# Chunk 0 of a recurrence with five idle products a pair instead of eight, and six weight tiles loaded in halves

## The chip, the core and the metric

The kernel runs on one NeuronCore of a Trainium2 chip. The metric is the time of one execution on the device in microseconds; before the change its median over three runs is 486.32 us. The engines are TensorE (PE, with its weight loads shown as PEld), VectorE (DVE), ScalarE (ACT), GpSimd (POOL) and SyncE (SP), which issues nearly all DMAs.

## What is computed

A linear recurrence over 768 tokens with a state of 48 x 48 for each of 4 x 8 heads, and behind it a two-layer network on its outputs:

```
for t in range(S):                              # S = 768
    cur = einsum('bhd,bhe->bhde', u * k[t], v[t])
    y[t] = einsum('bhd,bhde->bhe', r[t], state + cur)
    state = w * state + einsum('bhd,bhe->bhde', k[t], v[t])
x = y as (3072 tokens, 384)
h = x @ w_in                                    # 384 x 2048
g = maximum(h, 0) + alpha * minimum(h, 0)
out = g @ w_out                                 # 2048 x 384
```

All in float32. The kernel multiplies each float32 matrix as a sum of a high and a low half, three products for one (wh with xh, wl with xh, wh with xl).

## The kernel before

The tokens are cut into six chunks of 128 for each of the four batches (512 columns), the eight heads into four pairs. For each chunk, the recurrence of each pair is done with products inside the chunk and through a state carried from chunk to chunk; its output goes, split into xh and xl, into the tiles that the network reads. The network runs in steps: one step is one block of 128 of the 2048 hidden features for one chunk. A step issues nine products of the first matrix (`m_in`, L678), the leaky function on ScalarE and VectorE (L686 to L691), and nine products of the second matrix (`m_out`, L712) into three accumulators. Steps 0 to 8 are chunk 0 with weights 0 to 8, steps 9 to 17 chunk 1 with the same weights, steps 18 to 24 chunk 0 with weights 9 to 15, then the rest.

Weights arrive as 64-bit floats, 768 KB a block (`raw_weights`, L323, two buffers), and are turned into a high and a low float32 half by ScalarE and VectorE (`weights`, L343 to L354): L353 writes the high half, L354 the low one.

Chunk 0 (`first_chunk`, one call for each pair) runs before step 0: sums for the diagonal (L507, copied by L511), scores (L442), ScalarE's copies of a scaled identity (L449, eight a pair), VectorE's merging of the scores (L453), the outputs (L463) and, in `state`, transposes (L295, copied by L299) and state products (L489). The outputs of a pair are split by L389, L390 and L392, those of the last pair by L378 and L379. The first pair has its outputs in a tile of its own, from which `lower` (L367) moves twelve strips of 16 rows to where the products of step 0 read them: k = 0, 1, 2, high and low, two each, on SP's queue.

An idle product multiplies the identity by itself into the accumulator acc2, which nobody reads (`warm`, L233). `with_warm(n, ...)` issues n of them ahead of a group of real products, and a piece of 23 stands at the program's start.

The order of the instructions on each engine is not written by hand. Every piece of work is added with an engine, a cost in microseconds, its reads and writes and a rank, and the planner (`in_order`) places them one after the other by these costs, which include 0.16 for an idle product; where a hole of more than 0.25 us is left on TensorE ahead of the network, it fills it with idle products. So a change of an early cost can move work on all engines. Each of the engines then executes its queue in order.

DMAs take eight completion semaphores in turn (DMAHW0 to DMAHW7); a DMA waits for the one eight places before it. At the end, in the branch that is taken when the check of the inputs passed (the line number is that of the `If`, L840), SP waits for each of the eight, from DMAHW0 to DMAHW7, one instruction each, and then goes to the closing barrier. The check itself is a product (L775) and a few VectorE operations, up to L781.

## Time and profile before

| | us |
|---|---|
| median of three runs (lowest, highest) | 486.32 (486.30, 486.80) |
| the profiled execution, on the device | 486.93 |
| its span, from the first to the last instruction | 485.2 |
| TensorE busy | 476.6 (98%) |
| VectorE busy | 310.8 (64%) |
| ScalarE busy | 247.2 (51%) |
| GpSimd busy | 43.5 (9%) |

An engine's busy time counts its instructions from start to end. TensorE's are pipelined, so a row's duration there holds some overlap with the next; the distance from one row's start to the next row's start is what it takes in the queue. In a timeline the text in brackets is the idle time of the engine before the row and what ended it.

### The profile page before, as it was taken

The numbers are of one execution on the slowest core, as the hardware profiler recorded it, in microseconds if no ns is written. First come the engines' busy times: TensorE is split into PE (matmuls) and PEld (weight loads), VectorE is DVE, ScalarE is ACT, GpSimd is POOL, SyncE is SP. The second block draws the span as 40 slices with busy tenths as digits, with TensorE's granted clock in tenths as the row PEclk, the third lists the DMA queues.
The fourth block names the chain that finished last, engine by engine and source line by source line (L and its number), as shares of the span: only waits on it lengthen the run. The fifth ranks groups of instructions, "written<-read, shape, count | busy, mean of one in ns | idle before, by whom it ended". The sixth has DMA issues, their size and how long they took to land.

```text
span 485.2 us, 11237 instructions
## 1 busy us (share of the span) xinstructions
PE 476.6 (98%) x4644; PEld 387.5 (80%) x4644; DVE 310.8 (64%) x518; ACT 247.2 (51%) x578; POOL 43.5 (9%) x49
## 2 busy tenths in 40 slices
PE   8999999999999999999999999999999999999994
PEld 5778878888888888888888888888888878888883
DVE  7789999999786785855755655745644534333331
ACT  5889866776555552553553643444642333433222
POOL 2000010012211011101202202202000000000000
PEclk9999999999999999999999999999999999999998
DMA  8675776642243641431121341121210000100002
GB/s 238 193 209 187 225 242 190 228 157 66 72 131 106 187 136 57 136 103 36 58 83 37 118 119 37 54 75 33 95 26 1 1 1 0 67 0 0 1 1 70
DMA packets 23752, 45.82 MB, mean 94 GB/s; under 512 B 3856, under 2 KB 11408, under 8 KB 23696
## 3 DMA queue, kind: packets, MB, share of 16 engines
q1 hardware_dynamic: 23552, 44.92, 29.6%
q8 instruction: 38, 0.62, 0.6%
q14 instruction: 18, 0.15, 0.1%
q10 hardware_dynamic: 144, 0.13, 0.1%
HBM read 36.38 MB, written 6.29 MB: 88 GB/s over the span
## 4 chain that ended last, share of the span: by engine, by line
PE 88%; DVE 7%; ACT 2%; DMA 1%; issue 1%; POOL 0%; ACTq 0%; DVEq 0%; POOLq 0%
PE acc L712 40%; PE bank L678 38%; PE bank L612 2%; PE acc L233 2%; PE bank L622 2%; PE bank L591 2%; PE bank L584 1%; DVE wl L354 1%; DMA wraw<-wall 1%; DVE wx L350 1%; DVE wx L347 1%; DVE g L687 1%; DVE wx L345 1%; DVE gl L691 1%; ACT wx L343 1%
## 5 line engine op out<-in xcount | busy, mean ns | idle before, releaser
L687 DVE SCALAR_TENSOR_TENSOR g<-bank,alph,g 128x512 f32<-128x512 f32 x96 | 71.9, 748 | 107.0 <-ACT g L686 106.3
L686 ACT ACTIVATE g<-bank 128x512 f32<-128x512 f32 x96 | 57.3, 597 | 137.0 <-PE bank L678 136.5
L678 PE MATMUL bank<-xh,wh 128*128 128x512 f32 x288 | 113.0, 392 | 0.0
L678 PE MATMUL bank<-xh,wl 128*128 128x512 f32 x288 | 112.2, 390 | 0.1
L678 PE MATMUL bank<-xl,wh 128*128 128x512 f32 x288 | 112.1, 389 | 0.0
L691 DVE TENSOR_TENSOR gl<-g,gh 128x512 fp32r<-128x512 f32 x96 | 69.5, 724 | 41.6 <-ACT gh L690 41.4
L690 ACT ACTIVATE gh<-g 128x512 fp32r<-128x512 f32 x96 | 60.5, 630 | 66.1 <-DVE g L687 65.9
L712 PE MATMUL acc<-gh,wh 128*128 128x512 f32 x288 | 83.6, 396 | 0.0
L712 PE MATMUL acc<-gh,wl 128*128 128x512 f32 x288 | 82.0, 391 | 0.0
L712 PE MATMUL acc<-gl,wh 128*128 128x512 f32 x288 | 81.7, 390 | 0.0
L678 PEld LDWEIGHTS bank<-xh,wh 128*128 128x128 f32 x288 | 54.0, 188 | 11.6 <-ACT kk L299 0.3
L678 PEld LDWEIGHTS bank<-xh,wl 128*128 128x128 f32 x288 | 54.1, 188 | 11.5 <-DVE wl L354 0.5
L678 PEld LDWEIGHTS bank<-xl,wh 128*128 128x128 f32 x288 | 54.1, 188 | 11.3
L712 PEld LDWEIGHTS acc<-gl,wh 128*128 128x128 f32 x288 | 54.0, 188 | 11.3
L712 PEld LDWEIGHTS acc<-gh,wl 128*128 128x128 f32 x288 | 53.8, 188 | 11.4
L712 PEld LDWEIGHTS acc<-gh,wh 128*128 128x128 f32 x288 | 52.7, 188 | 11.2
L547 POOL TENSOR_TENSOR rr<-rr,kk 128x384 f32<-128x384 f32 x16 | 22.5, 1405 | 286.2 <-DMA kk<-vkr 227.1
L558 ACT ACTIVATE base<-ident,cu 128x64 f32<-128x64 f32 x160 | 41.5, 337 | 1.0 <-DVE cu L553 0.9
L379 DVE TENSOR_TENSOR xl<-bank,xh 48x256 fp32r<-48x256 f32 (+1 forms) x66 | 28.4, 430 | 1.5
L533 DVE TENSOR_TENSOR raw<-raw,W 112x512 f32<-112x512 f32 x40 | 26.7, 682 | 0.8 <-DMA raw<-rk 0.8
L378 ACT ACTIVATE xh<-bank 48x256 fp32r<-48x256 f32 (+1 forms) x66 | 25.5, 386 | 2.5 <-PE bank L622 1.0
L643 DVE COPY_PREDICATED base<-strict,bank 128x256 f32<-128x256 uint8 x40 | 17.3, 442 | 4.4 <-PE bank L591 4.4
(102 smaller groups left out, 388.2 us busy)
## 6 DMA issues: line engine op xcount, KB each, us to landing
wraw<-wall SPq DMA_DIRECT2D x16, 768.0 KB, 4.7
raw<-rk SPq DMA_DIRECT2D x46, 224.0 KB, 3.9
v<-vkr SPq DMA_DIRECT2D x24, 192.0 KB, 3.6
rr<-vkr SPq DMA_DIRECT2D x16, 192.0 KB, 2.5
kk<-vkr SPq DMA_DIRECT2D x16, 192.0 KB, 3.4
oT<-o SPq DMA_DIRECT2D x12, 256.0 KB, 2.2
oT<-g SPq DMA_DIRECT2D x5, 256.0 KB, 2.8
xh<-xh SPq DMA_DIRECT2D x36, 32.0 KB, 2.0
```

Of the source, the lines that this page charges most:

```text
L378: add("ACT", us, lambda: nc.scalar.activation(to(h), view(), AF.Copy), r=[src], w=refs(h), rank=rank)
L379: add("DVE", us + 0.1, lambda: nc.vector.tensor_tensor(out=to(l), in0=view(), in1=to(h), op=ALU.subtract), r=[src] + refs(h), w=refs(l), r ...
L533: add("DVE", 0.72, lambda t=t, tab=tab: nc.vector.tensor_tensor(out=t().rearrange("p b (j t) -> p (b j) t", t=span), in0=t().rearrange("p ...
L547: add("POOL", 1.2, lambda: nc.gpsimd.tensor_tensor(out=rt(), in0=rt(), in1=k(), op=ALU.mult), r=[k] + ([wh[12]] if c == 2 else []), w=[rt] ...
L558: add("ACT", 0.32, lambda g=g, b=b: nc.scalar.activation(base()[:, g, b], ident2(), AF.Copy, scale=cu()[:, g, b:b + 1]), r=[cu, ident2], w ...
L643: add("DVE", 0.42, lambda g=g: nc.vector.copy_predicated(base()[:, g], strict2()[:, None, :].broadcast_to([128, B, HI]), A[g]()[:, 0:256]. ...
L678: nc.tensor.matmul(hp()[:, :], a[i]()[:, k], x[c]()[:, k], start=(k == 0 and j == 0), stop=(k == NK - 1 and j == 2))
L686: add("ACT", 0.6, lambda: nc.scalar.activation(g(), hp()[:, :], AF.Copy), r=[hp], w=[g], rank=n - 100)
L687: add("DVE", 0.75, lambda: nc.vector.scalar_tensor_tensor(out=g(), in0=hp()[:, :], scalar=alph()[:, i:i + 1], in1=g(), op0=ALU.mult, op1=A ...
L690: add("ACT", 0.64, lambda: nc.scalar.activation(gh(), g(), AF.Copy), r=[g], w=[gh], rank=n - 100)
L691: add("DVE", 0.73, lambda: nc.vector.tensor_tensor(out=gl(), in0=g(), in1=gh(), op=ALU.subtract), r=[g, gh], w=[gl], rank=n - 99)
L712: nc.tensor.matmul(banks[k](), a[i]()[:, NK + k], x(), start=(begin and j == 0), stop=(end and j == 2))
```

## The change

Three things are changed. In `first_chunk`, `with_warm` gets 1 instead of 2 for the scores and for the outputs, and 0 instead of 1 for the state products; the sums for the diagonal keep 2, the transposes 1. The opening piece issues five idle products of 512 columns, one into each of the five rotating banks, and then 16 of 384 into acc2, instead of 23 of 384; the helper is split into `idle` and `warm` for that. And weights 10 to 15 are loaded by two DMAs of 384 KB each instead of one of 768 KB.

In the changed program 43 idle products are issued instead of 55: 41 by these parameters, and two that the planner puts ahead of the first transposes of chunk 1 (L295), of which two groups now stand ahead of step 0 instead of one. Ahead of every step's first product TensorE's queue otherwise holds the same products as before from step 3 on, apart from a few that change places with a neighbour, and apart from the check's product, which now stands far behind them. Lines of the changed file are higher by 3 to 10.

```diff
--- before.py
+++ after.py
@@ -229,9 +229,12 @@
 
 
     def warm(into):
-        x = ident().bitcast(mybir.dt.bfloat16)
-        nc.tensor.matmul(into()[:, 128:512].rearrange("p (a f) -> p a f", a=2), x[:, 0:128],
-                         x[:, None, 0:192].broadcast_to([128, 2, 192]), start=True, stop=True, skip_group_check=True)
+        idle(into()[:, 128:512])
+
+    def idle(into):
+        x, n = ident().bitcast(mybir.dt.bfloat16), into.shape[1] // 2
+        nc.tensor.matmul(into.rearrange("p (a f) -> p a f", a=2), x[:, 0:128],
+                         x[:, None, 0:n].broadcast_to([128, 2, n]), start=True, stop=True, skip_group_check=True)
 
     def with_warm(n, us, fn, r, w, rank):
 
@@ -320,8 +323,14 @@
 
     def raw_weights(i, rank, behind=()):
         t = raws[i] = sb([128, 2 * DM, 2], "wraw", 2, U32)
-        p = load(t, lambda: nc.sync.dma_start(t().rearrange("p f a -> p (f a)"), wall[i].bitcast(U32)), 768, rank, behind)
-        return p
+        if i < NF - 6:
+            return load(t, lambda: nc.sync.dma_start(t().rearrange("p f a -> p (f a)"), wall[i].bitcast(U32)), 768, rank,
+                        behind)
+
+        for j in range(2):
+            load((t, j), lambda j=j: nc.sync.dma_start(
+                t()[:, DM * j:DM * (j + 1)].rearrange("p f a -> p (f a)"),
+                wall[i].bitcast(U32)[:, 2 * DM * j:2 * DM * (j + 1)]), 384, rank)
 
     def weights(i, need):
 
@@ -442,7 +451,7 @@
                     nc.tensor.matmul(A[g]()[:, b * L:(b + 1) * L], k0()[half(g), b], r()[half(g), b], start=(b == 0),
                                      stop=(b == B - 1), skip_group_check=True)
 
-        with_warm(2, 1.05, scores, r=[r, k0], w=A, rank=q - 90).after.add(first)
+        with_warm(1, 1.05, scores, r=[r, k0], w=A, rank=q - 90).after.add(first)
         base = [sb([128, B, L], "gl", 3, F32, mv) if q % 2 else sb([128, B, L], "base", 3) for _ in range(2)]
         for g in range(2):
             for b in range(B):
@@ -464,7 +473,7 @@
                         :, x * D:x * D + rows.stop - rows.start], base[g]()[:, b], start=b == 0,
                         stop=b == B - 1, skip_group_check=True)
 
-        last_out[:] = [with_warm(2, 0.95, out, r=[v] + base, w=[y], rank=q - 85)]
+        last_out[:] = [with_warm(1, 0.95, out, r=[v] + base, w=[y], rank=q - 85)]
         h, l, kx = x_tiles(0, q)
         if q < P - 1:
             splits_by_pe(kx, h, l, y, 0.6, q - 51.2)
@@ -489,7 +498,7 @@
                         nc.tensor.matmul(u_rows(U, 0)[rows, b], kt[:, x * D:x * D + rows.stop - rows.start], v()[:, x],
                                          start=(b == 0), stop=(b == B - 1), skip_group_check=True)
 
-            with_warm(1, 0.75, product, r=[k, v], w=[U], rank=-45 + q)
+            with_warm(0, 0.75, product, r=[k, v], w=[U], rank=-45 + q)
             T[q] = sb([112, B, D], "T", 9)
             add("ACT", 0.4, lambda t=T[q]: nc.scalar.activation(t(), u_rows(U, 0), AF.Copy, scale=w128()[:, q:q + 1]),
                 r=[U, w128], w=[T[q]], rank=0.5 * q + 0.2)
@@ -781,7 +790,8 @@
         add("DVE", 0.1, lambda: nc.vector.tensor_copy(flag(), total()), r=[total], w=[flag], rank=at)
 
 
-    add("PE", 6.7, lambda: [warm(bank) for _ in range(23)], r=[ident], w=[(bank, "warm")], rank=-1000)
+
+    add("PE", 6.7, lambda: [idle(t) for t in plan.banks] + [warm(bank) for _ in range(16)], r=[ident], w=[(bank, "warm")], rank=-1000)
 
     begins = {}
     for n, (c, i) in enumerate(STEPS):
```

The first place is ScalarE's queue in chunk 0, from the copies for the third and fourth pair on: L449 (L458 after) is the scaled identity, L389 (L398) the first split of an output, L299 (L302) the copy of transposes, L343 (L352) and L353 (L362) belong to weights 0. Before:

```order
L449 ACTIVATE base<-ident,cu 128x128
L449 ACTIVATE gl<-ident,cu 128x128 x4
L389 ACTIVATE xh_394<-bank_116 112x512
L343 ACTIVATE wx<-wraw 128x768
L449 ACTIVATE gl<-ident,cu 128x128 x2
L299 ACTIVATE kk<-bank_118 128x192 x2
L449 ACTIVATE gl<-ident,cu 128x128 x2
L389 ACTIVATE xh<-bank_117 112x512
L389 ACTIVATE xh<-bank_119 112x512
L299 ACTIVATE kk<-bank_120 128x192 x2
L353 ACTIVATE wh_81<-wx 128x768
L299 ACTIVATE kk<-bank_118 128x192 x2
```

After:

```order
L458 ACTIVATE gl<-ident,cu 128x128 x4
L352 ACTIVATE wx<-wraw 128x768
L458 ACTIVATE base<-ident,cu 128x128 x4
L458 ACTIVATE gl<-ident,cu 128x128 x3
L302 ACTIVATE kk<-bank_119 128x192 x2
L302 ACTIVATE kk<-bank_120 128x192 x2
L458 ACTIVATE gl<-ident,cu 128x128
L398 ACTIVATE xh_441<-bank_117 112x512
L398 ACTIVATE xh<-bank_118 112x512
L398 ACTIVATE xh<-bank_116 112x512
L401 ACTIVATE xl_468<-bank_117 112x512
L401 ACTIVATE xl<-bank_118 112x512
```

Ahead of the first split, L389 or L398, stand 28 copies of the scaled identity before and all 32 after, and the six copies of transposes of the first three pairs and weights 0's first copy have moved ahead of it too.

The second place is SP's queue from the first strip of chunk 0 on: L367 (L376) moves a strip, xh high and xl low; wraw is a load of weights, raw, v and rr are inputs of chunk 1 and 2. Before:

```order
L367 DMA xh<-xh_394 16x512 x4
L323 DMA wraw<-wall 128x1536
L367 DMA xh<-xh_394 16x512
L404 DMA raw<-rk 112x512
L367 DMA xh<-xh_394 16x512
L367 DMA xl<-xl_469 16x512 x6
L406 DMA v<-vkr 128x384 x2
L404 DMA raw<-rk 112x512 x2
L406 DMA v<-vkr 128x384 x2
L323 DMA wraw<-wall 128x1536
```

After:

```order
L413 DMA raw<-rk 112x512 x3
L327 DMA wraw<-wall 128x1536
L376 DMA xh<-xh_441 16x512 x4
L376 DMA xl<-xl_468 16x512 x2
L376 DMA xh<-xh_441 16x512
L376 DMA xl<-xl_468 16x512 x2
L376 DMA xh<-xh_441 16x512
L376 DMA xl<-xl_468 16x512 x2
L415 DMA v<-vkr 128x384 x4
L554 DMA rr<-vkr 128x384
L327 DMA wraw<-wall 128x1536 x3
```

The loads of chunk 1's inputs and of weights 2 have left the places between the strips; the twelve strips follow each other.

The third place is SP's last stores, with the semaphores that each waits for (the DMA semaphore named is also the one that the store then takes; the store of the other half of the last tile is on ScalarE's queue and takes the semaphore between, DMAHW0 before and DMAHW6 after). Before:

```order
L755 DMA oT<-o 128x512 [waits DMAHW3_49,Activation_49]
L755 DMA oT<-o 128x512 [waits DMAHW4_49,Activation_49]
L755 DMA oT<-g 128x512 [waits DMAHW5_49,Activation_49]
L755 DMA oT<-o 128x512 [waits DMAHW6_49,Activation_49]
L755 DMA oT<-o 128x512 [waits DMAHW7_49,Activation_49]
L748 DMA oT<-g 128x256 [waits DMAHW1_49,DVE_49]
```

After:

```order
L764 DMA oT<-o 128x512 [waits DMAHW1_49,Activation_49]
L764 DMA oT<-o 128x512 [waits DMAHW2_49,Activation_49]
L764 DMA oT<-g 128x512 [waits DMAHW3_49,Activation_49]
L764 DMA oT<-o 128x512 [waits DMAHW4_49,Activation_49]
L764 DMA oT<-o 128x512 [waits DMAHW5_49,Activation_49]
L757 DMA oT<-g 128x256 [waits DMAHW7_49,DVE_49]
```

The last two stores take DMAHW0 and DMAHW1 before, DMAHW6 and DMAHW7 after.

## Rows read from the trace of the kernel before

**Rows 1.** Busy time by stage: stretch, its us, engines busy (instructions), clock, DMA share, GB/s.

```profile
8.00:30.90 22.90, 22.90 (x316) 16.54 (x315) 18.81 (x33) 19.88 (x60) 0.00 (x0) 1.00 0.73 218
30.90:70.00 39.10, 38.43 (x626) 30.74 (x625) 38.66 (x62) 31.86 (x82) 2.23 (x2) 1.00 0.72 232
70.00:478.00 408.00, 408.00 (x3680) 336.80 (x3679) 247.84 (x411) 191.18 (x426) 38.54 (x30) 1.00 0.23 72
```

**Rows 2.** Timeline of the opening: start us, us, engine, line, operation, count, [idle before].

```profile
1.48 6.58 PE L233 MATMUL acc<-ident 128*128 128x384 bf16 x25 [1.48 <-POOL ident L257]
...
5.94 0.15 PEld L233 LDWEIGHTS <-ident 128*128 128x128 bf16 x1 [0.17 <-issue]
...
6.26 1.42 PEld L233 LDWEIGHTS <-ident 128*128 128x128 bf16 x9 [0.17 <-issue]
```

**Rows 3.** Timeline of TensorE (PE) in chunk 0 and step 0.

```profile
10.51 0.50 PE L233 MATMUL acc<-ident 128*128 128x384 bf16 x2
10.94 0.63 PE L507 MATMUL acc<-uw,g 112*64 112x2 f32 x16
...
21.13 0.55 PE L295 MATMUL bank<-ident,raw 112*128 112x112 f32 x4
...
28.52 0.34 PE L233 MATMUL acc<-ident 128*128 128x384 bf16 x1
28.78 0.67 PE L489 MATMUL bank<-v,kk 128*64 128x48 f32 x16
...
32.88 0.39 PE L678 MATMUL bank<-xl,wh 128*128 128x512 f32 x1
```

**Rows 4.** Timeline of ScalarE (ACT) in chunk 0.

```profile
12.25 2.15 ACT L449 ACTIVATE gl<-ident,cu 128x128 f32<-128x128 f32 x7
...
17.10 0.99 ACT L449 ACTIVATE base<-ident,cu 128x128 f32<-128x128 f32 x3 [0.91 <-PE bank L463]
18.58 0.18 ACT L511 ACTIVATE cu<-acc 128x8 f32<-128x8 f32 x1 [0.50 <-PE acc L233]
...
20.12 0.58 ACT L389 ACTIVATE xh<-bank 112x512 fp32r<-112x512 f32 x1
20.59 0.91 ACT L343 ACTIVATE wx<-wraw 128x768 f32<-128x768 f32 x1
...
21.99 0.52 ACT L299 ACTIVATE kk<-bank 128x192 f32<-128x192 f32 x2
```

**Rows 5.** Timeline of VectorE (DVE) and TensorE where weights 1 are first used.

```profile
32.13 0.69 DVE L533 TENSOR_TENSOR raw<-raw,W 112x512 f32<-112x512 f32 x1
...
33.60 0.95 DVE L354 TENSOR_TENSOR wl<-wx,wh 128x768 fp32r<-128x768 f32 x1
...
34.67 0.50 PE L678 MATMUL bank<-xh,wh 128*128 128x512 f32 x1
```

**Rows 6.** SP's issues (timeline); part 6 of the page: KB each, us to landing.

```profile
20.72 3.01 SPq L367 DMA_DIRECT2D xh<-xh  x4
...
26.56 3.78 SPq L367 DMA_DIRECT2D xl<-xl  x6
...
226.93 4.93 SPq L404 DMA_DIRECT2D raw<-rk  x2
...
xh<-xh SPq DMA_DIRECT2D x36, 32.0 KB, 2.0
```

**Rows 7.** Windows of L678 alone; one line's view of L354 (min/median/max ns, starts).

```profile
0.00:121.60 121.60, 41.21 (x162) 29.98 (x163) 1.00 0.62 194
121.60:150.50 28.90, 13.21 (x54) 10.14 (x55) 1.00 0.36 115
...
L354 DVE TENSOR_TENSOR wl<-wx,wh x16: 942/950/1759, 25.3 to 123.3; 128x768 fp32r<-128x768 f32 x16
```

**Rows 8.** The tail: SP's waits (us in total, times, longest); its instructions of line 840.

```profile
SPq L840 <- SPq L840: 3.3, 2, 3.0
...
L840 SPq EVENT_SEMAPHORE  x8: 17/17/17, 483.1 to 483.9; - x8
```

## The prediction

> **What bounds the kernel now.** I read the windows first, because a share of 98% for TensorE says nothing about which stage could be shortened. From 8.0 to 30.9 us, the stage in which chunk 0 goes through the recurrence, TensorE is busy in all of its 22.90 us; from 30.9 to 70 it is busy for 38.43 of 39.10; from 70 to 478 for 408.00 of 408.00 [rows 1]. So the end of the program is the sum of what TensorE issues, plus a stall of well under a microsecond, plus the tail behind the last product. Whatever leaves TensorE's queue and is not replaced by a wait shortens the run, wherever it stands.
>
> The second thing to see in the windows is who would be late next. VectorE is busy for 18.81 of 22.90 us in chunk 0 (4.1 us idle) and for 38.66 of 39.10 between 30.9 and 70: after chunk 0 it is full, and it is the engine that makes the weights' low halves. One pair of rows shows how close it runs: the low half of weights 1 is written from 33.60 for 0.95 us, to 34.55, and the step that multiplies by it starts at 34.67 [rows 5]. So TensorE is full, but with VectorE right behind it, and ScalarE in chunk 0 (19.88 of 22.90) not far off.
>
> Third, the timeline of TensorE in chunk 0: between nearly all groups of real products stand idle products into acc2, one or two. Fourth, the tail: SP's own waits behind the last store.
>
> **The change, part by part.**
>
> *Idle products.* The parameters give 2+2+2+1+1 = 8 a pair before and 2+1+1+1+0 = 5 after, so 12 fewer over four pairs. The price: two of them take 0.43 us (10.51 to 10.94); one alone between two groups of small products takes 0.26 (28.52 to 28.78) [rows 3]; so the second of two is worth 0.17, and the first carries the cost of the interruption. Eight are "second of two", four (the state products) are whole interruptions: 8 x 0.17 + 4 x 0.26 = 2.4 us off TensorE's queue. The planner now sees one gap and fills it with two idle products ahead of the transposes of chunk 1; if TensorE waits there anyway, they cost nothing, otherwise 0.43. The other end of the term is that none of the 2.4 us reaches the end.
>
> *What is late next in chunk 0.* ScalarE's order changes with the planner's times [the first order listing above]. Ahead of its first split of an output, L389, at 20.12 now, stand 28 of the copies L449; in the changed order all 32 do, and also six copies L299 and one weights copy L343. At 2.15 us for seven copies, 0.52 for two L299 and 0.91 for L343 [rows 4], that is 4 x 0.31 + 3 x 0.52 + 0.91 = 3.7 us more work ahead of L389. Against it stands ScalarE's waiting for TensorE before that point, 0.91 at 17.10 and 0.50 at 18.58 [rows 4]; TensorE's groups come sooner now, so I let about 1.0 of it go. The first L389 then starts near 20.12 + 3.7 - 1.0 = 22.8 us (22.4 if all the waiting goes, 23.8 if none), and ends at 23.4.
>
> SP may then lower the strips: twelve transfers of 32 KB. Before, the first four were issued from 20.72 and the last six from 26.56 for 3.78 us, 0.63 each, the last of them beginning at 29.7; a strip lands in 2.0 us, at 31.7 [rows 6]. That was early enough: step 0's ninth product, the one that needs the last low strip, started at 32.88 [rows 3]. In the changed order the twelve follow each other without another load between them [the second listing], so the last begins at 23.4 + 11 x 0.63 = 30.3 and lands at 32.3. Without any wait TensorE would want it at 32.88 - 2.4 + 0.3 = 30.8, the 0.3 being a second transpose group of chunk 1 that is moved ahead of step 0 (0.55 with its pipelined end [rows 3], so 0.4 in the queue), less the check's product, which leaves. So the strip ends this wait, and step 0's ninth product can come only about 0.5 us sooner than before; with the transposes already done that is 0.9 us of work gained, and some 1.5 turned into waiting.
>
> *VectorE behind it.* For the 0.9 to be kept, the low halves must keep up. Ahead of the low half of weights 3 stands exactly the same VectorE work in both orders, so it comes sooner by what VectorE idles less in chunk 0. Of its 4.1 us idle [rows 1] most are waits for ScalarE's L449 copies, which are released sooner; the wait for the second weights' copy stays. I take 1.2 us less idling, enough for 0.9 from weights 3 on. Weights 1 may even be late, since two scalings L533 (0.69 [rows 5]) and one product L500 of the same size now stand ahead of it: 3 x 0.7 = 2.1 us more. With 1.2 less idling weights 1 come 0.9 later; that is the bad end, 0.9 us lost.
>
> So for chunk 0 and what follows: between 2.4 gained and 0.9 lost; I take **0.9 gained**, the value at which the strips leave it, because the strips' rows are the nearest.
>
> *The opening.* 23 idle products of 384 columns become 5 of 512 and 16 of 384: 8,832 columns become 8,704. They are 0.32 us apart until 6.26 us and 0.16 after, nine in 1.42 [rows 2]; 128 columns are 0.05 us at the second rate and 0.11 at the first. I take 0.05.
>
> *Halves of weights 10 to 15.* Six more issues of at most 0.5 us on SP, and a ScalarE copy that waits for two landings. By 121.6 us TensorE has issued 162 products of the first matrix, 18 steps of nine, and step 18 is the first that needs weights 9; the last of the sixteen low halves is begun at 123.3, while 54 products more, to step 24 which needs weights 15, take until 150.5 [rows 7]. With some 26 us in hand the halves cost nothing at TensorE. If that cover were gone, it would be one issue a weight, 6 x 0.5 = 3 us. The check's last operations move back to some 227 us, and SP's read of the flag with them, in between two loads of which the second is held by its buffer for most of 4.93 us [rows 6]: nothing.
>
> *The tail.* Behind the last store SP waits for the eight DMA semaphores one by one. Before, the two last stores hold the first and second of them: the two waits that cost something are 3.0 and 0.3 us, and the eight instructions run from 483.1 to 483.9 [rows 8]. So after the second, at 483.4, six waits that are long satisfied take 0.5 us before SP goes on to the closing barrier. Six more loads move the last two stores to the seventh and eighth semaphore [the third listing], and those six are passed while the stores are still under way. The saving is 0.5 (0.4 to 0.5, for the rows are rounded), and since SP is the last at the barrier it is on the path. It does not depend on chunk 0.
>
> **The sum.** 0.9 + 0.05 + 0.5 = 1.45 us. The profiled execution took 486.93 us (span 485.2 and 1.7 around it) and should become 485.5; the median of the runs, 486.32, is 0.6 lower, so 484.9.
>
> **TensorE's clock.** In the rows the opening shows both levels: 384 columns in 0.32 us are 1.2 GHz, in 0.16 us 2.4 GHz, and the rise came after 4.8 us of unbroken idle products [rows 2]; after that no group in chunk 0 is slowed, and the windows stand at 1.00. The Trainium skill ("TensorE: Matmul & The Clock Gate", Part 1: The HAM clock gate) says that the throttled level is the default and only activity releases it, and that a matrix engine left without work falls back. It speaks against taking idle products out. By it the changed stage might be paid in part at the low level; the trace of before has no spell on which to see it. That is the rival below.
>
> **The rivals.**
>
> 1. *TensorE keeps all of it.* If the strips or the last copies come sooner than I reckon (the bounds of L389 alone give 0.4), up to 2.4 + 0.05 + 0.5 = 2.95 us: 483.4. For it: TensorE had practically no stall, and every step is preceded by the same products as before, but for the idle ones. Against it: the strips' 0.63 each, and VectorE full from 30.9. Chance 0.18 for 483.4 to 484.2.
> 2. *Only the tail.* Weights 1 or 2 decide, and TensorE is where it was after step 2: 486.32 - 0.55 = 485.8; with the 0.9 lost, 486.7. For it: 0.12 us between the low half and its product. Against it: 4.1 us of idling that can shrink. Chance 0.28 for 485.4 to 486.7: no measurable change.
> 3. *The clock falls in chunk 0, slower than before.* Place: the waits ahead of step 0, where TensorE waits perhaps 1.5 us in two or three pieces with only small products between. If it falls to 1.2 GHz there, and needs again the 4.8 us of the opening, those 4.8 us bring work worth 2.4: 484.9 + 2.4 = 487.3; twice, 489.7. It decides from the first spell of more than 4.8 us on, since less still ends below 487.3. For it: fewer idle products, more waiting. Against it: between 30.9 and 70 us TensorE is without work for 0.67 us before, without harm [rows 1], and two products were put into the longest gap. Chance 0.10.
>
> **How the numbers follow.** The forecast, 0.44, has 484.2 to 485.4 as its own range. Measurement cannot tell less than about 0.2%, 0.97 us, from no change, so faster means below 485.35 and slower above 487.29. Faster: 0.43 of the forecast and 0.18 of rival 1, 0.61. Slower: rival 3, 0.10. The same: 0.01 and 0.28, 0.29. For 8 in 10 the range goes from rival 1's end, 483.4, past rival 2's bad end to 486.8; it leaves out rival 3 and the outermost of the first two.
>
> **What would show it.** In the changed profile: 43 idle products instead of 55; the first L389 near 22.8 and the last strip issued near 30.3; step 0's ninth product near 32.4 with a wait on a DMA ahead of it; the first product of weights 1 no sooner than 34 us, against 34.67; the eight waits at the end with the long one seventh and none behind the eighth. I am wrong if step 0's ninth product follows the eighth without a wait and comes 2 us sooner than 32.88 (rival 1), if a product of weights 1 or 2 is released by VectorE at 34.6 or later (rival 2), or if products of 512 columns in chunk 0 or step 0 stand 0.4 us apart (rival 3).

## The result: 489.3 us, slower by 0.67%

The changed kernel took 489.28 us (median of 8 executions, 487.6 to 493.0) against 486.31 for the kernel before (8 executions, 485.5 to 487.9): a ratio of 1.0067, with a 95% interval of 1.0043 to 1.0090. I had forecast 484.9 in a range of 483.4 to 486.8 and given "slower" one chance in ten. The executions spread over 5.4 us where those of before spread over 2.4, and four of the eight have a mean TensorE clock of 0.989 to 0.994; of 115 executions of the kernel before that stand beside the experiments, none is below 0.995. One more of these took 1216 us at a whole clock and is left out.

The profiled execution of the changed kernel is its fastest, 487.62 us (span 485.7). So two later traces of the same kernel are read beside it, one of 488.71 and one of 492.74 us.

### The profile page after: what moved, and what is told of

It reads as the page before. It is cut to its first block, busy times and chain, and to the rows that moved or that the text cites. A ratio compares the mean times of both kernels' runs of the same rounds, so it can differ in the third digit from the quotient of the medians.

```text
span 485.7 us, 11222 instructions
## 1 busy us (share of the span) xinstructions
PE 475.2 (98%) x4632; PEld 386.7 (80%) x4632; DVE 310.9 (64%) x518; ACT 247.0 (51%) x578; POOL 40.7 (8%) x49
## 4 chain that ended last, share of the span: by engine, by line
PE 92%; DMA 3%; ACT 3%; issue 0%; SPq 0%; POOL 0%; DVE 0%; ACTq 0%; POOLq 0%
PE acc L721 41%; PE bank L687 39%; DMA wraw<-wall 3%; PE bank L621 2%; PE bank L631 2%; PE bank L600 2%; PE bank L593 1%; PE acc L236 1%; ACT wx L352 1%; PE acc L516 0%; PE bank L236 0%; PE bank L451 0%; PE acc L451 0%; DMA xl<-xl 0%; ACT base L567 0%
## 5 line engine op out<-in xcount | busy, mean ns | idle before, releaser
L556 POOL TENSOR_TENSOR rr<-rr,kk 128x384 f32<-128x384 f32 x16 | 19.4, 1215 | 290.2 <-DMA kk<-vkr 176.2
L388 DVE TENSOR_TENSOR xl<-bank,xh 48x256 fp32r<-48x256 f32 (+1 forms) x66 | 28.4, 430 | 2.0 <-ACT xh L387 0.5
L542 DVE TENSOR_TENSOR raw<-raw,W 112x512 f32<-112x512 f32 x40 | 27.7, 712 | 0.2 <-DMA raw<-rk 0.2
```

Of the source, the lines that this page charges most:

```text
L388: add("DVE", us + 0.1, lambda: nc.vector.tensor_tensor(out=to(l), in0=view(), in1=to(h), op=ALU.subtract), r=[src] + refs(h), w=refs(l), r ...
L542: add("DVE", 0.72, lambda t=t, tab=tab: nc.vector.tensor_tensor(out=t().rearrange("p b (j t) -> p (b j) t", t=span), in0=t().rearrange("p ...
L556: add("POOL", 1.2, lambda: nc.gpsimd.tensor_tensor(out=rt(), in0=rt(), in1=k(), op=ALU.mult), r=[k] + ([wh[12]] if c == 2 else []), w=[rt] ...
```

## The profile after

By stage, from the windows view of the changed kernel (columns as in [rows 1]):

```profile
8.00:30.90 22.90, 21.81 (x306) 16.52 (x304) 20.45 (x36) 21.20 (x62) 0.00 (x0) 1.00 0.79 233
30.90:70.00 39.10, 36.99 (x615) 29.30 (x614) 36.22 (x58) 30.30 (x80) 2.23 (x2) 1.00 0.69 215
70.00:478.00 408.00, 408.00 (x3680) 336.47 (x3680) 248.81 (x412) 190.09 (x426) 35.82 (x30) 1.00 0.23 73
```

TensorE now idles 1.09 us in chunk 0 and 2.11 between 30.9 and 70, where before it idled 0.00 and 0.67. VectorE, full before in the second stage (38.66), works 36.22 of it: it waits as well. So what ends last is neither of them.

SP's waits between 10 and 40 us (total, times, longest), and its issues from the timeline:

```profile
SPq L413 <- PE bank L298: 5.0, 2, 4.8
SPq L376 <- DMA wraw<-wall: 2.1, 1, 2.1
```

```profile
15.45 6.87 SPq L413 DMA_DIRECT2D raw<-rk  x3
22.42 0.37 SPq L327 DMA_DIRECT2D wraw<-wall  x1
23.01 2.49 SPq L376 DMA_DIRECT2D xh<-xh  x4
25.60 1.17 SPq L376 DMA_DIRECT2D xl<-xl  x2
26.86 0.54 SPq L376 DMA_DIRECT2D xh<-xh  x1
29.50 1.14 SPq L376 DMA_DIRECT2D xl<-xl  x2
30.69 0.58 SPq L376 DMA_DIRECT2D xh<-xh  x1
31.32 1.21 SPq L376 DMA_DIRECT2D xl<-xl  x2
32.63 1.95 SPq L415 DMA_DIRECT2D v<-vkr  x4
```

The load of weights 2 goes out at 22.42, ahead of the twelve strips, right behind two raw loads that had waited 4.8 us for a bank of TensorE. It lands 7.1 us later, at 29.48. The strip after 26.86 goes out at 29.50, 2.1 us behind the end of the one before it: the queue stood and waited for that landing. The program's list of SP's instructions, with their waits, says why: the eight DMA semaphores are dealt out in turn, each transfer waits for the landing of the one eight before it, and this strip is the eighth behind the load. In the kernel before, the eighth transfer behind the same load is a strip too, but the load (out at 24.14) had landed at 28.81, just ahead of that strip's turn at 29.05, and nothing stood.

```
DMA wraw<-wall 128x1536 [waits DMAHW7_49,DVE_49,Activation_49]
...
DMA xl<-xl_468 16x512 [waits DMAHW7_49]
```

The Trainium skill (DMA: Bandwidth & Descriptors, section Why a DMA increments its semaphore by 16 and not by 1) gives the reason for such a wait: when two transfers in flight share one semaphore, a wait on its count can pass before the first of them has fully landed. No run here shows that; the trace shows the price.

What TensorE makes of it, from its timeline (answers to [rows 3, 5]):

```profile
29.25 0.98 PE L298 MATMUL bank<-ident,raw 112*128 112x112 f32 x8 [0.95 <-DVE xl L388]
30.32 0.47 PE L687 MATMUL bank<-xh,wh 128*128 128x512 f32 x1
...
32.05 0.50 PE L687 MATMUL bank<-xl,wh 128*128 128x512 f32 x1 [0.33 <-DMA xl<-xl]
32.71 0.50 PE L687 MATMUL bank<-xh,wh 128*128 128x512 f32 x1 [0.16 <-DMA xh<-xh]
...
34.07 0.47 PE L687 MATMUL bank<-xl,wh 128*128 128x512 f32 x1 [0.63 <-DMA xl<-xl]
35.28 0.63 PE L593 MATMUL bank<-v,kk 64*64 64x48 f32 x31 [0.74 <-ACT g L695]
...
37.30 0.47 PE L687 MATMUL bank<-xh,wh 128*128 128x512 f32 x1
```

The 0.95 ahead of the transposes is a wait for VectorE, which has still to write the low half of the last pair (L388) and so frees the bank late. Step 0 starts at 30.32, 0.60 sooner than before, and then waits three times for strips: its nine products take 3.75 us from first start to last where before they took 1.96. The ninth starts at 34.07, and the first burst behind it waits 0.74 once more. The view puts that down to a copy of ScalarE, but the instruction also waits for a v load that SP issued at 32.63, behind the strips, and that landed at 35.15. Step 1 starts at 37.30 (before 34.67), with more of chunk 1's work ahead of it; step 2 at 40.83 (before 39.41), 0.4 us of it for a group of transposes that the kernel before does later; step 5 at 64.83 (before 63.91). So chunk 0 and what follows have lost 0.9 us there.

## The experiments

Each was timed in rounds beside the kernel before on its chip, unless it says otherwise; the ratio is to that kernel. "Low clock" counts executions with a mean clock of 0.994 or less.

| Kernel | order | median us | ratio (95%) | low clock |
|---|---|---|---|---|
| changed, again | new | 489.16 | 1.0053 (1.0035 to 1.0070) | 3 of 12 |
| halves only | before | 486.34 | 0.9994 (0.9982 to 1.0007) | 0 of 12 |
| order kept | before | 486.38 | 0.9995 (0.9981 to 1.0009) | 3 of 12 |
| new order, 8 idle | new | 492.26 | 1.0133 (1.0113 to 1.0153) | 4 of 5 |
| load later | new | 488.25 | 1.0037 (1.0020 to 1.0055) | 0 of 12 |
| no load of weights 2 | new | 487.98 | 1.0038 (1.0021 to 1.0054) | 2 of 12 |
| waits filled | new | 488.36 | 1.0043 (1.0027 to 1.0060) | 0 of 12 |
| load by GpSimd | new | 488.33 | 1.0046 (1.0029 to 1.0062) | 2 of 11 |
| the same, no load of weights 7 | new | 487.20 | 1.0015 (1.0002 to 1.0029) | 3 of 11 |
| the same, split first | new | 486.88 | 1.0014 (1.0001 to 1.0027) | 3 of 12 |
| split first | new | 488.61 | 1.0053 (1.0034 to 1.0073) | 3 of 6 |
| order kept, split first | before | 486.37 | 0.9986 (0.9974 to 0.9999) | 6 of 11 |
| order kept, split first, filled | before | **485.23** | **0.9962 (0.9950 to 0.9975)** | 0 of 5 |
| before, split first | before | 486.71 | 0.9994 (0.9984 to 1.0005) | 0 of 12 |
| load by GpSimd, split first, filled | new | 488.02 | 1.0035 (1.0017 to 1.0053) | 1 of 12 |

**1. The halves alone.** The new `raw_weights` in the kernel before.

> The kernel before with weights 10 to 15 loaded in halves and nothing else changed. The tail theory: the last two stores use the seventh and eighth semaphore, so the long wait at the end is the seventh and nothing is left behind the eighth: 0.5 us less, 485.8 where before is 486.3. Rival: the twelve smaller loads disturb the middle of the program, or the end hangs on something else than these waits: no change or slower, 486.3 to 487.

The median, 0.35 us under that of the kernel before beside it (486.69), can't tell. The traces can: from the landing of the last store to the end of the span it is 1.83 us in the kernel before (483.39 to 485.22) and 1.39 here (484.58 to 485.97). The tail's term holds, 0.45 us. The profile after has the same 1.38 us behind its last landing at 484.35; SP's waits there, and the line's instructions, answer to [rows 8]:

```profile
SPq L850 <- SPq L850: 2.6, 3, 1.8
...
L850 SPq EVENT_SEMAPHORE  x8: 17/17/17, 481.8 to 484.4; - x8
```

The eighth of the waits now stands at 484.4, where the last store has just landed, and no satisfied wait follows it.

**2. The order kept.** The planner is told the old numbers, and fewer products are issued.

```
-    def with_warm(n, us, fn, r, w, rank):
+    def with_warm(n, us, fn, r, w, rank, do=None):
...
-        ... [warm(bank) for _ in range(n)] + [fn()] ...
+        ... [warm(bank) for _ in range(n if do is None else do)] + [fn()] ...
...
+        with_warm(2, 1.05, scores, ..., do=1)   # out: 2, do=1; product: 1, do=0
```

> All three parts of the change, but the planner still reckons with eight idle products a pair, so that every other instruction stands in the order of before; 12 idle products less are issued. Theory 1 (the new order did the harm: it puts the load of weights 2 ahead of the strips, and the eighth transfer behind that load waits for its landing on the DMA semaphore that they share): that wait is not there, and 0.5 of the tail and 0.5 to 2 us of chunk 0 are gained: 483.5 to 485.5. Theory 2 (fewer idle products do the harm, by waits of TensorE after which its clock falls): slower than before as the changed kernel is, 487.5 or more, with some executions at a mean clock of 0.989.

Neither, as it stands: no loss and no gain in the median. Its waits of TensorE:

```profile
PE bank L298 <- ACT T L503: 0.7, 1, 0.7
PE bank L498 <- ACT kk L302: 0.7, 1, 0.7
PE bank L516 <- DVE g L509: 0.4, 1, 0.4
PE bank L472 <- ACT kk L302: 0.2, 1, 0.2
```

The trace has step 0's ninth product at 31.83 (before 32.88). So some 1.0 us of the idle products' 2.4 arrives, and 1.6 goes into three new waits for ScalarE's copies (0.7, 0.7 and 0.2). These are the forecast's amounts, 0.9 and 1.5, but by luck: it had the strips at the end of the wait, in the new order. What hides the gain in the median is in experiment 7.

**3. The new order with the old idle products.** `do=2, 2, 1` at the new numbers.

> The order of the changed kernel, with the idle products of the kernel before put back at their places (eight a pair, 67 in all with the opening and the two fills taken as they are in the changed kernel). Theory 1: the strips' wait stays, TensorE's extra 2.4 us of idle products fall in its waits ahead of step 0; the time stays at the changed kernel's, 487.5 to 490. Theory 2: with the idle products back the clock holds and the time goes back to that of before or below, 485.8 to 486.5, and no execution shows a mean clock of 0.989.

Theory 2 as I had put it falls: idle products alone don't bring the time back; theory 1's 487.5 to 490 is missed as well. (The trace has 55 idle products, as the kernel before; the 67 in the expectation was a miscount.) The order costs 1.3% with eight of them and 0.5 to 0.7% with five, so in this order taking them out *gains* 3 to 4 us. How much of that is the clock is open: it falls in four of these five executions. In the windows view of its trace:

```profile
37.70:41.10 3.40, 3.40 (x11) 2.73 (x10) 2.47 (x5) 2.55 (x7) 0.00 (x0) 0.50 0.93 320
```

(Columns as in [rows 1]; the clock, third from the end, is 0.50 for these 3.4 us.)

**4. The load of weights 2: moved, left out, on another queue.**

```
+    order.insert(order.index(sixth strip) + 1, loads[2])          # load later
+    return load(t, (lambda: setattr(t, "t", raws[1]())) if i == 2 else ...   # no load of weights 2
+    return load(t, lambda: (nc.gpsimd if i == 2 else nc.sync).dma_start(...  # load by GpSimd
```

> The changed kernel with one instruction moved: the load of weights 2 is issued behind the first six strips instead of ahead of all twelve. Theory 1: the 2.1 us wait of a strip for that load's landing goes, the last strip is issued near 30 us instead of 31.9, step 0's ninth product comes near 32 to 32.5 instead of 34.1, and the time falls by 1.5 to 2.5 us against the changed kernel's: 486 to 487.5, with less spread. Theory 2: nothing changes, 488 to 493 as the changed kernel.

> The changed kernel without the load of weights 2: weights 1 are split once more in their place, so the output is not the reference's; every other instruction and its order are those of the changed kernel. Theory 1 (the load stands ahead of the strips: one strip waits for its landing on the shared semaphore, the others land behind it, and the v loads of chunk 1 come late because SP's queue stands): step 0's ninth product comes near 32.3 instead of 34.1, the first burst of chunk 1 behind it no longer waits 0.7, step 1 starts near 35 instead of 37.3, and the time is 2 to 3 us below the changed kernel's: 486 to 487.5. Theory 3 (the new order of TensorE and ScalarE itself loses the time, with the second transposes and the products L516 ahead of steps 0 and 1): step 1 still at 36.5 or later, 488.5 to 490.

> The changed kernel with the load of weights 2 issued by GpSimd, on a queue and a semaphore of its own, and not by SP; nothing else moves. Theory 1: no strip waits for it on a semaphore and none queues behind it, the last strip is issued near 30 and not 31.9, and the time falls to 486.5 to 488. If the strips are late because the load takes the bandwidth and not because of queue and semaphore, they land as late as in the changed kernel and the time stays at 489. Theory 3: 489 too.

The strips' wait on SP for the load goes in all three; what TensorE gets of it differs. Without the load, step 0's nine products take 2.05 us again. On GpSimd's queue the last strip goes out at 30.03, the ninth product comes at 32.16, and step 5 starts at 63.12, where the changed kernel needs until 64.83 and the kernel before until 63.91. With the load behind six strips the last strip goes out at 30.57, but the six behind the load land only with it, from 32.23 to 33.06 (load 31.99), and TensorE waits 1.41 for one of them: the nine products still take 3.58 us, and the ninth comes at 33.58 instead of the expected 32 to 32.5. And the time hardly follows in any of them: 488.0 to 488.3, and theory 1's 486 was wrong for the sum. The trace with GpSimd's queue shows where the 1.7 us went (timelines of ScalarE and TensorE):

```profile
65.03 0.89 ACT L352 ACTIVATE wx<-wraw 128x768 f32<-128x768 f32 x1 [2.23 <-DMA wraw<-wall]
65.94 0.60 ACT L398 ACTIVATE xh<-bank 112x512 fp32r<-112x512 f32 x1
...
66.59 0.48 PE L399 MATMUL bank<-xh,minus 112*112 112x512 f32 x1 [1.81 <-ACT xh L398]
```

ScalarE waits 2.23 us for the landing of weights 7 (at 65.00). That load had gone out at 57.44, 1.96 sooner than in the profile after, but took 7.56 us where it took 5.26 there. Behind that copy in its queue stands the split L398, whose input had been ready since about 63.2, and TensorE, whose next product L399 needs the split, waits 1.81 in the middle of step 5. The profile after has the same three rows, at other times:

```profile
64.69 0.93 ACT L352 ACTIVATE wx<-wraw 128x768 f32<-128x768 f32 x1 [0.18 <-DMA wraw<-wall]
65.64 0.60 ACT L398 ACTIVATE xh<-bank 112x512 fp32r<-112x512 f32 x1
...
66.33 0.46 PE L399 MATMUL bank<-xh,minus 112*112 112x512 f32 x1
```

In the eight traces of the new order in which these places are untouched, step 10 starts 23.8 to 24.0 us behind the landing of weights 7, however chunk 0 went: 64.66 and 88.55 in the profile after, 68.52 and 92.38 in experiment 3, 65.00 and 88.83 here. In the kernel before (64.81 and 87.69) and with the order kept (63.86 and 86.75) it is 22.9. In seven of the eight TensorE waits for the split, by 0.25 to 2.10 us; in the profile after it comes to the split's product just when the split is done, and does not wait. So at some 65 us a load can set the program, and the new order stands 1.0 us worse towards it. Whether it does depends on how long the load takes: the issue follows what was gained before it, the landing need not.

These are single traces, and chunk 0 differs between executions: two more kernels with the load on GpSimd's queue and an untouched chunk 0 (experiment 5) come to step 5 at 64.47 and 64.48.

*What is lost behind step 10.* From step 10 to the last step every trace of the new order agrees with the others to 0.04 us, and every trace of the order of before with the others, but the new order takes 0.37 us longer. All of it lies in step 40, into which the planner has moved the check's product. After (first fence) and before (second), TensorE's timeline from step 40's ninth product to the next step's first:

```profile
227.28 0.39 PE L687 MATMUL bank<-xl,wh 128*128 128x512 f32 x1
227.59 0.20 PE L784 MATMUL bank<-ok,one 128*1 128x20 f32 x2
...
229.91 0.39 PE L687 MATMUL bank<-xh,wh 128*128 128x512 f32 x1
```

```profile
226.41 0.39 PE L678 MATMUL bank<-xl,wh 128*128 128x512 f32 x1
...
228.68 0.39 PE L678 MATMUL bank<-xh,wh 128*128 128x512 f32 x1
```

That is 2.63 us against 2.27. Ahead of step 0 the same product took 0.13 (30.79 to 30.92 in the kernel before).

**5. Does that wait take the gain?** Without the load of weights 7 (weights 6 used twice), and, nothing left out, with two places of the order changed.

```
+    return load(t, (lambda: setattr(t, "t", raws[6]())) if i == 7 else ...   # no load of weights 7
+    # split first: ScalarE's split and high half of weights 6 ahead of its copy of weights 7,
+    # VectorE's low half of weights 6 ahead of its first shift of weights 7
+    order.remove(made_w[7][0]); order.insert(order.index(made_w[6][4]) + 1, made_w[7][0])
+    ahead(made_w[6][5], made_w[7][1])
```

> The kernel with the load of weights 2 on GpSimd's queue (step 5 started at 63.1 us there, 1.7 sooner than in the changed kernel, and then TensorE waited 1.8 at 66.6 for ScalarE's split, which stands behind the copy of weights 7 as loaded), now without the load of weights 7: weights 6 are split once more in their place, so the output is not the reference's. Theory 4 (what is gained or lost in chunk 0 is levelled at some 65 us, since TensorE's queue there is tied to the landing of weights 7): the wait at 66.6 goes, step 10 starts at 86.5 to 87.2 instead of 88.8, and the time falls by 1.6 to 2.3 us, to 486 to 486.8. Rival (the order of TensorE's work loses it elsewhere): no more than 0.5 us gained.

> The kernel with the load of weights 2 on GpSimd's queue, and beside it two places in the order of ScalarE and VectorE changed near 65 us: ScalarE makes the split and the high half of weights 6 ahead of its first copy of weights 7, and VectorE the low half of weights 6 ahead of its first shift of weights 7. Nothing is left out. Theory 4: TensorE no longer waits there for the landing of weights 7, step 10 starts at 86.5 to 87.3 and the time is 486 to 487, at or just below the kernel before. Rival: weights 7 themselves come too late for step 7, or the wait moves to another place: 488 to 488.5.

> The changed kernel with the same two moves near 65 us alone (the load of weights 2 stays with SP, ahead of the strips). Theory 4: its step 5 starts near 64.8, so step 10 can come at 88.1 to 88.3 instead of 88.6 to 89.1, and the executions in which the landing of weights 7 is late are cut: 488 to 488.7 where the changed kernel has 489.2. Theory 1 alone: no change, 489.2.

With the load on GpSimd's queue both edits bring the ratio from 1.0046 to 1.0015 and 1.0014, and no wait of L399 is left in either trace. The traces don't show the step 10 that I expected (86.5 to 87.3): it is at 88.11 and 88.77, for their chunk 0 is late, in the second with 3.4 us of low clock from 35.6, and there a wait of 0.57 us has moved to 74.8. So the gain is shown by the ratios alone. Alone, with the load of weights 2 where the change put it, the moves bring nothing that can be told: 1.0053, step 10 at 88.92, and its three executions of a whole clock have a mean of 488.4, where those of the changed kernel run beside experiment 6 have 488.7. So neither edit alone (1.0046, 1.0053) comes to what both do, as theory 4 has it. Of the 0.7 us that are left, by the traces 0.37 is the check's product, and 0.18 the tail: with one load fewer in SP's turn the last stores take the sixth and seventh semaphore, and from the last landing to the end it is 1.56 us instead of 1.38 in the second trace.

**6. The clock.** Fourteen idle products in the waits of the changed kernel.

```
+FILLS, FIRST, MORE = {(0, 1, 2): 2, (0, 2, 2): 4}, 4, 4   # step 0's 6th, 9th product; first burst; transposes
```

> The changed kernel with 14 idle products more, put where TensorE waits in its trace: four ahead of the transposes of chunk 1, two and four ahead of the sixth and ninth product of step 0, four ahead of the first burst of chunk 1. Theory 2 (part of the loss is a fall of the clock behind those waits, as the trace of the kernel with the new order and eight idle products showed between 37.7 and 41.1 us): no execution with a mean clock of 0.992 or less, the slowest executions (491 to 493) vanish, the median goes from 489.3 to about 488.5. Theory 1 alone, without a part of the clock: no gain, 489 to 490, since the idle products only take the place of the waits or add to them.

> The changed kernel once more, beside these, for more executions and a second trace. Theory 1: a strip waits again for the landing of the load of weights 2, 1 to 3 us, and step 2 starts 1.4 to 3 us later than in the kernel before. Theory 2: among the executions some have a mean clock of 0.992 or less and are 2 to 4 us longer than the others; the median stays at 489 to 489.5.

> The changed kernel, for a third trace: a strip waits for the landing of the load of weights 2, the first burst of chunk 1 for a v load, and step 10 starts 23.8 to 24.0 us behind the landing of weights 7, whatever the execution's time is; 487.5 to 490.

As theory 2 has it: no low clock in twelve executions, against 7 of the 20 timed ones of the changed kernel. Those 7 average 491.0 us, the other 13 488.7, so by estimate the clock is 0.8 us of the loss on average (0.35 x 2.3), as much as the filled kernel's median is lower. It is not all of the spread: the two slowest of the filled kernel, 490.4 and 491.3, have a whole clock, where I expected the slowest to vanish. Step 2 comes 0.9 us later than in the kernel before in the changed kernel's second trace (I expected 1.4 to 3), 4.8 in the third. The third (one execution, 492.74 us, over the 490 that I expected) caught a fall of the clock. Windows, and TensorE's and ScalarE's timelines:

```profile
30.90:35.60 4.70, 2.91 (x13) 1.34 (x13) 3.76 (x6) 2.76 (x8) 0.00 (x0) 1.00 0.44 123
35.60:42.50 6.90, 6.90 (x92) 6.10 (x93) 3.90 (x6) 2.73 (x8) 0.00 (x0) 0.51 0.84 307
42.50:50.00 7.50, 7.50 (x162) 6.15 (x161) 6.29 (x11) 6.86 (x20) 0.00 (x0) 1.00 0.03 8
```

```profile
30.68 0.47 PE L687 MATMUL bank<-xh,wh 128*128 128x512 f32 x1 [0.89 <-DMA xh<-xh]
...
34.32 0.47 PE L687 MATMUL bank<-xl,wh 128*128 128x512 f32 x1 [0.63 <-DMA xl<-xl]
35.57 1.01 PE L593 MATMUL bank<-v,kk 64*64 64x48 f32 x31 [0.77 <-ACT g L695]
...
40.10 0.63 PE L687 MATMUL bank<-xl,wh 128*128 128x512 f32 x1
40.53 0.63 PE L687 MATMUL bank<-xh,wh 128*128 128x512 f32 x1
...
42.57 0.39 PE L687 MATMUL bank<-xl,wh 128*128 128x512 f32 x1
42.80 0.86 PE L721 MATMUL acc<-gh,wh 128*128 128x512 f32 x3
...
69.49 0.89 ACT L352 ACTIVATE wx<-wraw 128x768 f32<-128x768 f32 x1 [2.13 <-DMA wraw<-wall]
70.40 0.60 ACT L398 ACTIVATE xh<-bank 112x512 fp32r<-112x512 f32 x1
...
71.05 0.49 PE L399 MATMUL bank<-xh,minus 112*112 112x512 f32 x1 [1.72 <-ACT xh L398]
```

Behind waits of 0.89, 0.22, 0.17, 0.63 and 0.77 us in step 0 the clock is at half, 1.2 GHz, from 35.6 to 42.5 us: products of 512 columns take 0.43 us from start to start, then 0.23 again. With all of it later, the load of weights 7 goes out at 62.55, where the profile after has 59.40, and lands at 69.46; L399 waits 1.72, and step 10 starts at 93.35, 23.89 behind the landing.

**7. The best version.** The order kept, split first, and then its two waits filled with four idle products each.

> The kernel in the order of before with twelve idle products less, the opening and the halves (486.4, not to be told from before), with the same two moves near 65 us. Theory 4: there TensorE lost only 0.4 us to the landing of weights 7 (0.1 ahead of the split's product, 0.24 in step 6), so 0.3 to 1 us: 485.4 to 486.1, the best of all and 0.6 to 1 below before. Rival: those waits only pass to step 7, whose low half was ready 0.6 ahead: 486.4.

> The kernel in the order of before with twelve idle products less and the two moves near 65 us (its executions fell in two groups: 484.0 to 485.4 with a mean clock of 0.996 and more, 486.4 to 486.8 with 0.993; its trace shows 3.4 us at half clock from 30.9 us on, behind two waits of 0.7), now with eight idle products put into these two waits, four in each (4 x 0.17 = 0.68 us). Theory 2 (the fewer idle products let the clock fall in some executions): all executions at 0.995 or more, one group, median 484.9 to 485.3, 0.3% below before. Rival (the clock's fall comes from something else): again two groups and 486.4, or 0.7 to 1.4 slower because the idle products delay TensorE.

> The kernel before with the two moves near 65 us alone. Theory 4: TensorE lost 0.43 us to the landing of weights 7 in its trace (0.21 ahead of the split's product at 67.1, 0.22 ahead of the second product of step 6), so 485.9 to 486.2, 0.2 to 0.5 below before. Rival: no change, 486.4.

Unfilled, the median misses the expected 485.4 to 486.1, since the executions fall in two groups: five at 484.0 to 485.4, six at 486.4 to 486.8 with a clock of 0.993. The windows view shows the trace of the second group (first fence) and the filled kernel (second):

```profile
30.90:34.40 3.50, 3.50 (x11) 2.62 (x10) 3.22 (x5) 1.80 (x6) 0.00 (x0) 0.51 0.77 213
```

```profile
30.90:34.40 3.50, 3.50 (x77) 2.89 (x76) 3.47 (x6) 3.03 (x8) 0.00 (x0) 1.00 0.64 191
```

Eight idle products in waits of 0.7 us leave one group in its five executions, 484.5 to 485.4, and the fastest kernel of all, 0.25 to 0.5% under the kernel before. The moves alone bring the kernel before nothing that can be told: the wait ahead of the split's product, 0.21 us in its trace, is gone, but one of 0.23 stands at 73.3 instead.

**8. All three undone in the new order.**

> The changed kernel with all three causes undone: the load of weights 2 on GpSimd's queue, the two moves near 65 us, and eleven idle products in the three waits of 0.95, 0.57 and 0.82 us around step 0. If these three are the whole loss, no execution has a mean clock below 0.995 and the median is 485.9 to 486.4 (486.9 without the idle products, of which three executions in twelve were at 0.992 to 0.994). If something else is left in the new order, it stays at 486.9 or more.

> The last kernel in the new order (load of weights 2 on GpSimd's queue, two moves, waits filled) once more, for a second trace: its executions ran from 485.9 to 490.7 with the clock whole, and the one traced was the fastest. If a late landing makes the slow ones, this trace shows a wait of TensorE between 66 and 85 us behind a load of weights that took over 7 us, or chunk 0 begun late (its first product after 8 us, or a raw load landing later than 21 us); if there is none of these and the time is still over 487.5, the loss lies where no theory has it.

> The same, for a third trace: the same signs as in the second.

The profiled execution came at 485.85, but the median is 488.0: something is left. In the second trace (one execution, 488.55 us) it is the same kind of wait one load later, on ScalarE's copy of weights 8 (landed at 74.55):

```profile
74.63 0.89 ACT L352 ACTIVATE wx<-wraw 128x768 f32<-128x768 f32 x1 [1.19 <-DMA wraw<-wall]
75.55 0.16 ACT L647 ACTIVATE seen_y<-bank 1x2 f32<-1x2 f32 x1
...
75.77 0.69 PE L631 MATMUL bank<-base,v 64*48 64x64 f32 x16 [1.06 <-ACT seen_y L647]
```

The third (486.97) shows it again, 1.07 us; the first, of the fastest execution, has 0.07. Beside it stand the check's 0.37 and the tail's 0.18, as in experiment 5. Together these three, 1.6 us, are of the size of what the median has over the kernel before beside it (1.36 us), but three traces can't say how often the wait comes. An execution of over 490 us at a whole clock was not caught in a trace; what makes those stays open.

## Why the prediction was wrong

*Idle products: right.* 43 are left. In the order of before the trace divides their 2.4 us into the forecast's amounts, by luck (experiment 2).

*ScalarE's order: right.* The first L398 (before: L389) starts at 22.38; I had 22.8 with 22.4 as its lower end.

*The strips: this step failed.* "The twelve follow each other without another load between them, so the last begins at 23.4 + 11 x 0.63 = 30.3 and lands at 32.3." It began at 31.95 and landed at 33.93, and step 0's ninth product came at 34.07 instead of 32.4. I counted the issues between the strips and not the transfer put ahead of them, though my own listing showed it, and took SP's waits to be only for data. With the load on GpSimd's queue the step comes out as I had reckoned: last strip out at 30.03, landed at 32.02, ninth product at 32.16. What the step lacked is the 2.1 us that SP stood for the load. With it went "1.5 turned into waiting": in the profile after TensorE waited 2.1 us up to the ninth product and 0.74 more behind it, and the "0.9 gained" was 0.9 lost at step 5.

*Weights 1: the wrong rival.* Step 1 started at 37.30 and was not released by VectorE; the low half that I had priced as the danger was not what was late.

*What lies behind 40 us: missing.* I followed the gain to step 1 and took it to the end of the program unchanged, since TensorE's windows are full. The chain of waits of the kernel before runs over VectorE from 30.0 to 60.0 us, and then over the load that lands at 64.81 (chain view of before):

```profile
60.03 4.78 DMA wraw<-wall
```

I did not ask what that load would do to a gain or a loss from chunk 0. In the new order it took away the gain of the trace with GpSimd's queue and kept the losses. It does not always: with the order kept it goes out 0.92 sooner (59.11), takes 4.75, and step 10 comes 0.94 sooner.

*The check: put at nothing, measured 0.37.* "The check's last operations move back to some 227 us": I priced SP's read of the flag there, and not what the check's product does to TensorE's queue between two steps. It costs 0.37 us there and had cost 0.13 ahead of step 0.

*VectorE: right in chunk 0, lost behind it.* It idles 2.45 us there instead of 4.09 (I had 1.2 less), and 2.9 instead of 0.4 between 30.9 and 70.

*The tail: right*, 0.45 for 0.5. *The opening:* real products start 0.29 sooner in this trace, but the clock's rise differs by more than that between traces (4.6 to 7.5 us from the start), so 0.05 is neither shown nor refuted.

*Rival 3: right in kind, too small in chance.* The clock does fall behind the new waits of step 0, in a third of the executions. I gave it 0.10 and made it the only way to a slower kernel; most of the loss needs no fall. Its price of 2.4 us is near the 2.3 by which those executions are longer, but from a spell of 4.8 us that no trace has: the falls lasted 3.4 or 6.8. The Trainium skill (TensorE: Matmul & The Clock Gate, Part 1: The HAM clock gate), weighed there, says that a matrix engine left without work falls back to the low level; these traces agree, 0.50 from 37.7 to 41.1 us in experiment 3, behind waits of 0.64 and 0.74. The idle time of the kernel before, 0.67 us, was no evidence against it: its longest single wait is 0.35 us, and each trace with a fall has two or more waits of 0.57 us or longer ahead of it. Such waits are not enough, though: the profile after has them (0.63, 0.74) and stays at 1.00.

## What to carry to other kernels

A count that feeds a planner is an edit of the whole order: price the order first, everything that moves in it, hold it fixed in an experiment, and only then price the instructions removed. Ask of each large transfer that moves ahead of small ones what waits for it, the queue and its semaphores included, and follow a gain through the longest transfers on the chain of waits to the end, for there it can be lost. Filler taken out of a busy engine's queue gains only where no wait takes its place; put back into two waits, eight products of 0.17 us went with a median lower by over 1 us.

## What the runs showed of the hardware

- Strips of 32 KB issued behind a 768 KB load on the same queue landed in order behind it: issued from 23.01, they landed from 29.66, the load at 29.48. With the load on GpSimd's queue (landed at 28.51) all but the first still landed from 28.83 on; only SP's wait for it was gone.
- A load of 768 KB (weights 2 and 7 in the traces that load them) took 4.5 to 7.7 us from issue to landing.
- A fall of the clock lasted 3.4 us in four traces (experiments 3, 5 and 7) and 6.8 in one, at half the rate, and hit only some executions of one program.
